# The second matrix product of an attention-and-MoE kernel as Strassen's seven half-size products

## The chip, the cores and the metric

One core of one Trainium2 chip. The metric is the device time of one execution of the whole kernel in microseconds (us); the median of several runs is compared. A core has TensorE (PE, matrix products into PSUM), VectorE (DVE, elementwise), ScalarE (ACT, activation functions), GpSimd (POOL, here used to issue loads that also convert types) and SyncE (SP, here used to issue stores and transposing transfers). Each engine takes its own instructions in the order of the program, and engines wait for one another through semaphores.

## The reference

```python
# q, k, v: (8, 8, 576, 64) = batch, heads, sequence, head_dim;  chunks of 64 along the sequence
scores = (1 / sqrt(64)) * q_c @ k_c.T            # 64 x 64 for each chunk and head
attn   = softmax(scores)
out    = attn @ v_c
x      = out as (4608 tokens, 512)
h      = x @ w_in                                # 512 -> 2048
g      = h * sigmoid(beta * h)
return g @ w_out                                 # 2048 -> 512, float32
```

Two matrix products of equal size, 4608 x 512 x 2048 each, hold nearly all of the arithmetic.

## The kernel before, in words

**Tiling.** The 4608 tokens are 18 units of 256 tokens; two units make a block of 512 tokens, so there are nine blocks (0 to 8). For each unit: loads of q, k (`load_qk`, L95 and L101) and v (`load_v`, L109) on GpSimd's queue, converted to fp16; a transpose of q and k (`emit_T`), on VectorE for units 0 to 7 (L153) and as transposing transfers on SP for units 8 to 17 (L148); the scores on TensorE and their exponential on ScalarE (`emit_sc`; units from 8 on: matmul L208, exp L214); the product with v (`emit_pv`, L242), whose extra 65th column, a constant in the v tile, gives the softmax denominators; the division on VectorE (`emit_norm`, reciprocal L253 and multiply L257); and the transpose of the result to `xt` (`emit_xt_pe`, or `emit_xt_dma` on SP, L281).

**First layer** (`emit_m(j, m)`): for block j and each of 16 slices m of 128 columns of w_in, four matmuls of 512 columns (L292) into one PSUM bank `hps`, a tanh on ScalarE (L300) and one VectorE operation (L301) that writes g in fp16 to `gt`, 128 x 16 x 512. It uses h * sigmoid(beta h) = 0.5 h (tanh(beta h / 2) + 1), with `beta2` = beta/2 (L369); the factor 0.5 is applied when the output is copied.

**Second layer** (`emit_t(j, t)`): for each 128 tokens t of block j, 16 matmuls of 512 columns (L314) with a slice of `gt` as the weights and `w_out16` as the moving operand; then a copy with scale 0.5 on ScalarE (L324) and a store on SP (L326). The very last 128 tokens are done in two halves of 256 columns (L478).

**Memory.** PSUM's eight banks: four in `ps_p` (hps, ops and the PE transposes), two in `ps_s` (scores, and the second half of pv), two in `ps_x` (the first half of pv). `qk_p` has four buffers, so the load of unit u + 4 into a q or k buffer waits until unit u has been transposed. `qt_p` has two. v is kept whole in `vbig`, 36 tiles of 128 tokens.

**Order.** The program is recorded by hand (`tc.manual_schedule()`). Blocks 0 and the start of 1 are written out. From there, for each j a list of items with a position between 0 and 1 (and a priority for ties) is sorted and emitted: the m of block j, the second layer of block j - 1, and the attention of the two units of block j + 1. For the attention `att_items(u, a0, w)` places sc at `a0`, pv at `a0 + 0.40 w`, the norms behind it and `T(u+1)`, with w the share of the block that the unit has (0.43 from j = 3 on, a0 = 0.03 and 0.46). emit_T(u) also records the loads of unit u + 4 behind it, on GpSimd.

```python
        def att_items(u, a0, w):
            return [(a0, 2, ("sc", u)), (a0 + 0.40 * w, 3, ("pv", u)),
                    (a0 + 0.41 * w, 3, ("norm", u, 0)), (a0 + 0.55 * w, 3, ("norm", u, 1)),
                    (a0 + (0.70 if u + 1 < XU else 0.10) * w, 3, ("T", u + 1))]
```

Of the kernel before, what the change touches and what calls it, by code (L numbers as in the profile page):

```python
# [8 lines left out]
FP32 = mybir.dt.float32  # L9
FP16 = mybir.dt.float16  # L10
# [5 lines left out]
def kernel(  # L16
# [18 lines left out]
    NU = NT // UNIT  # L35
    NTILE = NT // 128
    VP = 80
    scale = 1.0 / float(D) ** 0.5

    const = ctx.enter_context(tc.tile_pool(name="const", bufs=1))  # L40
# [22 lines left out]
    beta2 = const.tile([128, KFF], FP32)  # L63
# [43 lines left out]
    def load_v(i):  # L107
        for off, n, b, s in runs(i * 128, 128):
            nc.gpsimd.dma_start(  # L109
                out=vbig[off:off + n, i, :, 0:D],  # L110
                in_=v[b, :, s:s + n, :].rearrange("h p d -> p h d"),
            )

# [116 lines left out]
            nc.scalar.activation(out=et[:, s], in_=sc[:, s], func=ACTF.Exp, scale=scale)  # L230
        et_t[u] = et

    def emit_pv(u):
        et = et_t.pop(u)
        for s in range(2):
            i = 2 * u + s
            pool, tag = ((ps_x, "x"), (ps_s, "s"))[s]
            x = pool.tile([128, 2, 4, 128], FP32, tag=tag, name="x")
            for g in range(4):
                for r in range(2):  # L240
                    for c in range(2):
                        nc.tensor.matmul(  # L242
                            out=x[64 * c:64 * c + 64, r, g, 0:D + 1],
                            lhsT=(et[64 * r:64 * r + 64, s, 4 * c + g, :] if u < XU else
                                  et[64 * r:64 * r + 64, g % 2, 4 * s + 2 * c + g // 2, :]),
                            rhs=vbig[64 * r:64 * r + 64, i, 4 * c + g, 0:D + 1],
                        )
            x_t[u, s] = x

# [35 lines left out]
    def emit_m(j, m, c0=0, n=None):  # L285
        n = blocks[j][1] * UNIT if n is None else n
        if j not in gt_t:
            gt_t[j] = gt_p.tile([128, KFF, 512], FP16, tag="gt", name="gt")
        hps = ps_p.tile([128, 512], FP32, tag="p", name="hps")
        xr = xt_t[j].rearrange("p t (r k) (c q) -> p (t r) (k c) q", r=2, c=2)  # L290
        for kk in range(KDM):
            nc.tensor.matmul(  # L292
                out=hps[:, 0:n],
                lhsT=w_in16[m // 2][:, kk, (m % 2) * 128:(m % 2) * 128 + 128],
                rhs=xr[:, c0 // CH:(c0 + n) // CH, 2 * (kk % 2) + kk // 2, :],
                start=(kk == 0),
                stop=(kk == KDM - 1),
            )
        sg = sg_p.tile([128, 512], FP32, tag="sg", name="sg")
        nc.scalar.activation(out=sg[:, 0:n], in_=hps[:, 0:n], func=ACTF.Tanh, scale=beta2[:, m:m + 1])  # L300
# [7 lines left out]
    def emit_t(j, t, k0=0, k1=None):  # L308
        k1 = KFF if k1 is None else k1
        if k0 == 0:  # L310
            ops_t[j, t] = ps_p.tile([128, DM], FP32, tag="p", name="ops")
        ops = ops_t[j, t]
        for kk in range(k0, k1):
            nc.tensor.matmul(  # L314
                out=ops,
                lhsT=gt_t[j][:, kk, t * 128:(t + 1) * 128],
                rhs=w_out16[kk // 4][:, kk % 4, :],
                start=(kk == 0),
                stop=(kk == KFF - 1),
            )  # L320
        if k1 < KFF:
            return
        osb = osb_p.tile([128, DM], FP32, tag="osb", name="osb")
        nc.scalar.activation(out=osb, in_=ops, func=ACTF.Copy, scale=0.5)  # L324
        r0 = blocks[j][0] * UNIT + t * 128
        nc.sync.dma_start(out=out[r0:r0 + 128, :], in_=osb)  # L326

    def emit_idle(n, w):
        d = ps_p.tile([128, 512], FP32, tag="p", name="warm")
# [3 lines left out]
    with tc.manual_schedule():  # L333
        nc.vector.memset(idle, 0.0)
        nc.vector.memset(braw, 0.0)  # L335
        nc.vector.memset(vbig[:, :, :, D:D + 1], 1.0)
# [29 lines left out]
        emit_T_half(1)  # L366
        emit_sc_half(1)
        nc.vector.transpose(out=bt, in_=braw)
        nc.scalar.activation(out=beta2, in_=bt[:, 0:KFF], func=ACTF.Copy, scale=0.5)  # L369
        loads_to(4)  # L370
        emit_idle(8, 128)
        emit_pv(0)
# [23 lines left out]
        for s in range(4):  # L396
            for t in range(4):
                if s == 2 and t == 1:
                    emit_T(2)
                if s == 2 and t == 3:  # L400
                    emit_sc(2)
                if s == 3 and t == 0:
                    emit_pv(2)
                    emit_norm(2, 0)
                    emit_norm(2, 1)
                    emit_T(3)
                if s == 3 and t == 2:
# [14 lines left out]
        emit_m(1, 7, 0, 256)  # L422

        def att_items(u, a0, w):
            return [(a0, 2, ("sc", u)), (a0 + 0.40 * w, 3, ("pv", u)),
                    (a0 + 0.41 * w, 3, ("norm", u, 0)), (a0 + 0.55 * w, 3, ("norm", u, 1)),
                    (a0 + (0.70 if u + 1 < XU else 0.10) * w, 3, ("T", u + 1))]

        for j in range(1, NB):
            items = []  # L430
            if j == 1:
                items += [(0.04 * m, 0, ("h", m)) for m in range(8)]
                items += [(0.32 + 0.085 * (m - 8), 0, ("m", m)) for m in range(8, KFF)]
                items += [(0.80, 3, ("T", 4))]
            else:
                m0 = 0.30 if j == 2 else 0.02
                items += [(m0 + (1 - m0) * m / KFF, 0, ("m", m)) for m in range(KFF)]
                for t in range(4):
                    for hf in range(2):
                        items.append((0.98 * (t + 0.5 * hf) / 4, 1, ("t", t, hf)))  # L440
                if j == 2:
                    items += [(0.00, 0, ("sc", 4)), (0.05, 3, ("pv", 4)), (0.06, 3, ("norm", 4, 0)),
                              (0.07, 3, ("norm", 4, 1)), (0.08, 3, ("T", 5)), (0.13, 2, ("sc", 5)),
                              (0.16, 2, ("xp", 4, 0)), (0.18, 2, ("xp", 4, 1)), (0.20, 2, ("pv", 5)),
                              (0.21, 3, ("norm", 5, 0)), (0.22, 3, ("norm", 5, 1)), (0.23, 3, ("T", 6)),
                              (0.27, 2, ("xp", 5, 0)), (0.29, 2, ("xp", 5, 1))]
                if j + 1 < NB:
                    if j == 2:
                        items += att_items(6, 0.36, 0.32) + att_items(7, 0.68, 0.29)
                    else:  # L450
                        for i in range(2):
                            items += att_items(2 * j + 2 + i, 0.03 + 0.43 * i, 0.43)
            items.sort(key=lambda it: it[:2])
            for _, _, it in items:
                if it[0] == "m":
                    emit_m(j, it[1])
                elif it[0] == "h":
                    emit_m(j, it[1], 256, 256)
                elif it[0] == "t":
                    emit_t(j - 1, it[1], 8 * it[2], 8 * it[2] + 8)  # L460
                elif it[0] == "sc":
                    emit_sc(it[1])
                elif it[0] == "pv":
                    emit_pv(it[1])
                elif it[0] == "norm":
                    emit_norm(it[1], it[2])
                    if it[1] not in (4, 5):
# [7 lines left out]
        for hf in range(2):  # L475
            ops = ps_p.tile([128, DM], FP32, tag="p", name="ops")
            for kk in range(KFF):
                nc.tensor.matmul(  # L478
                    out=ops[:, 0:256],
                    lhsT=gt_t[NB - 1][:, kk, 384:512],  # L480
                    rhs=w_out16[kk // 4][:, kk % 4, 256 * hf:256 * hf + 256],
                    start=(kk == 0),
                    stop=(kk == KFF - 1),
                )
            osb = osb_p.tile([128, DM], FP32, tag="osb", name="osb")
            dst = out[NT - 128:NT, 256 * hf:256 * hf + 256]
            if hf == 0:
                nc.scalar.activation(out=osb[:, 0:256], in_=ops[:, 0:256], func=ACTF.Copy, scale=0.5)
                nc.sync.dma_start(out=dst, in_=osb[:, 0:256])
            else:  # L490
                nc.vector.tensor_scalar(out=osb[:, 0:256], in0=ops[:, 0:256], scalar1=0.5, scalar2=None, op0=ALU.mult)
                nc.scalar.dma_start(out=dst, in_=osb[:, 0:256])


# [28 lines left out]
```

## Time and profile before

| | |
|---|---|
| median of 3 runs | 298.5 us (298.28 to 300.6) |
| span of the profiled execution, first to last instruction | 296.9 us |
| PE, DVE, ACT, POOL busy | 282.6, 140.9, 148.4, 97.1 us |
| granted TensorE clock, mean | 0.988 of full |
| second layer's matmuls, 512 columns | 560 seen, L314 |
| landing of a transposing transfer, issue to landed, median | kT 7.5 us, qT 8.4 us, xt 2.9 us |
| landing of an output store of 256 KB, median | 3.8 us |

How to read it: matmuls are pipelined, so the mean duration of one (379 ns for 512 columns) is longer than the distance from one to the next; the chain of work that ended last, which gives the time that each stretch of matmuls adds, is the better measure. The profiled execution has no time of its own beside its span: the runs' times are taken apart from it, and lie around 1.6 us above the span.

### The profile page before, as it was taken

To read this page: it belongs to the slowest core of one execution; us is meant where nothing else is said; L and a number is where in the kernel's file an instruction comes from. 1 tells how busy PE (TensorE), PEld (TensorE's weight loads), DVE (VectorE), ACT (ScalarE), POOL (GpSimd) and SP (SyncE) were. 2 spreads that over 40 slices of the span, in tenths; PEclk is the share of its full clock that TensorE was granted. 3 is DMA by queue.
4 is the path that set the end of the run, shared out by engine and by line. 5 is a ranking of instruction groups with operands and counts; after the bars stand their busy time and mean duration, and the time that the engine had idled before them with its cause. 6 is when DMAs were issued, how large, how long until landed. Compare 5 with 4: busy or idle time off the path is not lost.

```text
span 296.9 us, 6545 instructions
## 1 busy us (share of the span) xinstructions
PE 282.6 (95%) x2722; PEld 139.2 (47%) x2722; DVE 140.9 (47%) x258; ACT 148.4 (50%) x232; POOL 97.1 (33%) x124
## 2 busy tenths in 40 slices
PE   7699999897799999999999999999999999999995
PEld 3565445644444444444444444444444444444444
DVE  3457604876547535353535353535353536444300
ACT  3278317872646554555455545554545454544411
POOL 8853678417934563324445151000000000000000
PEclk9869999999999999999999999999999999999999
DMA  9999999999996999999999999863527312100111
GB/s 141 165 197 205 182 179 209 206 122 74 172 149 96 149 188 134 144 148 151 140 153 155 143 130 148 126 112 62 121 72 110 56 57 75 48 35 35 38 71 71
DMA packets 141932, 36.86 MB, mean 124 GB/s; under 512 B 130000, under 2 KB 137424, under 8 KB 141904
## 3 DMA queue, kind: packets, MB, share of 16 engines
q0 software_dynamic: 101216, 18.10, 81.2%
q1 hardware_dynamic: 40544, 18.24, 32.0%
q8 instruction: 21, 0.34, 0.5%
q10 hardware_dynamic: 144, 0.13, 0.1%
q14 instruction: 7, 0.06, 0.1%
HBM read 36.71 MB, written 9.44 MB: 155 GB/s over the span
## 4 chain that ended last, share of the span: by engine, by line
PE 79%; DMA 10%; POOL 4%; DVE 2%; ACT 2%; issue 2%; DVEq 0%; ACTq 0%; POOLq 0%
PE ops L314 37%; PE hps L292 36%; DMA wout<-in_moe_w_out_dram 5%; DMA win<-in_moe_w_in_dram 3%; DMA qu<-in_q_dram 2%; PE x L242 2%; POOL vbig L109 2%; PE sc L208 1%; PE ops L478 1%; PE sc L221 1%; DVE x L257 1%; ACT xt L277 1%; POOL qu L101 1%; POOL ku L101 1%; POOL h L339 1%
## 5 line engine op out<-in xcount | busy, mean ns | idle before, releaser
L301 DVE SCALAR_TENSOR_TENSOR gt<-sg,hps 128x512 f16<-128x512 f32 (+1 forms) x158 | 100.6, 639 | 119.0 <-ACT sg L300 118.8
L292 PE MATMUL hps<-xt,win 128*128 128x512 f16 (+1 forms) x632 | 139.1, 365 | 2.6 <-ACT xt L277 2.2
L300 ACT ACTIVATE sg<-hps,beta 128x512 f32<-128x512 f32 (+1 forms) x158 | 101.9, 650 | 78.0 <-PE hps L292 77.4
L314 PE MATMUL ops<-wout,gt 128*128 128x512 f16 x560 | 130.9, 379 | 0.0
L292 PEld LDWEIGHTS <-win 128*128 128x128 f16 x632 | 60.8, 99 | 62.8 <-issue 2.8
L314 PEld LDWEIGHTS <-gt 128*128 128x128 f16 x560 | 53.8, 98 | 63.5
L324 ACT ACTIVATE osb<-ops 128x512 f32<-128x512 f32 x35 | 20.9, 597 | 40.8 <-PE ops L314 40.8
L95 POOL DMA_DIRECT2D qu<-in_q_dram x22 | 18.5, 850 | 62.9 <-DMA qT<-qu 46.2
L109 POOL DMA_DIRECT2D vbig<-in_v_dram x40 | 34.1, 869 | 10.4 <-DMA wout<-in_moe_w_out_dram 4.3
L257 DVE TENSOR_TENSOR x<-x,rd 128x512 f16<-128x512 f32 (+1 forms) x40 | 25.2, 637 | 1.2
L95 POOL DMA_DIRECT2D ku<-in_k_dram x22 | 18.7, 868 | 0.0
L230 ACT ACTIVATE et<-sc 128x1024 f16<-128x1024 f32 (+1 forms) x9 | 7.3, 833 | 14.6 <-PE sc L221 14.5
L253 DVE RECIPROCAL rd<-x 128x8 f32<-128x8 f32 x36 | 7.2, 201 | 12.9 <-PE x L242 12.9
L214 ACT ACTIVATE et<-sc 128x1024 f16<-128x1024 f32 x10 | 10.2, 1016 | 0.0
L242 PEld LDWEIGHTS <-et 64*64 64x64 f16 x576 | 6.3, 109 | 7.8 <-issue 2.5
L221 PE MATMUL sc<-qT,kT 32*64 32x64 f16 x448 | 5.3, 199 | 4.1 <-DVE qT L153 4.1
L242 PE MATMUL x<-vbig,et 64*64 64x65 f16 x576 | 8.4, 197 | 0.8 <-ACT et L230 0.6
L101 POOL DMA_DIRECT2D qu<-in_q_dram x10 | 7.7, 783 | 2.2 <-DMA win<-in_moe_w_in_dram 1.5
L101 POOL DMA_DIRECT2D ku<-in_k_dram x10 | 7.7, 774 | 2.1 <-DMA win<-in_moe_w_in_dram 1.3
L331 PE MATMUL warm<-idle 128*128 128x128 f16 (+1 forms) x42 | 6.9, 319 | 1.2 <-DVE braw L335 1.2
L221 PEld LDWEIGHTS <-kT 32*64 32x64 f16 x448 | 4.6, 112 | 6.9 <-DVE qT L153 4.2
L277 ACT COPY xt<-xp 128x512 f16<-128x512 f16 x10 | 5.6, 585 | 1.9 <-PE xp L273 1.9
(34 smaller groups left out, 58.0 us busy)
## 6 DMA issues: line engine op xcount, KB each, us to landing
out_dram<-osb SPq DMA_DIRECT2D x35, 256.0 KB, 3.8
vbig<-in_v_dram POOLq DMA_DIRECT2D x32, 128.0 KB, 7.4
qu<-in_q_dram POOLq DMA_DIRECT2D x20, 128.0 KB, 5.5
ku<-in_k_dram POOLq DMA_DIRECT2D x20, 128.0 KB, 6.8
win<-in_moe_w_in_dram POOLq DMA_DIRECT2D x8, 256.0 KB, 8.8
wout<-in_moe_w_out_dram POOLq DMA_DIRECT2D x4, 512.0 KB, 12.4
qu<-in_q_dram POOLq DMA_DIRECT2D x4, 256.0 KB, 6.0
ku<-in_k_dram POOLq DMA_DIRECT2D x4, 256.0 KB, 7.4
```

The source lines that it names most:

```text
L95: nc.gpsimd.dma_start(out=tv[off:off + n, sp], in_=src[b, :, s:s + n, :].rearrange("h p d -> p h d"),)
L101: nc.gpsimd.dma_start(out=t[off // 2:(off + n) // 2], in_=src[b, :, s:s + n, :].rearrange("h (p r) d -> p h r d", r=2),)
L109: nc.gpsimd.dma_start(out=vbig[off:off + n, i, :, 0:D], in_=v[b, :, s:s + n, :].rearrange("h p d -> p h d"),)
L214: nc.scalar.activation(out=et, in_=sc, func=ACTF.Exp, scale=scale)
L221: nc.tensor.matmul(out=sc[o0:o0 + 64, c // 2, h, :], lhsT=kt[p0:p0 + 32, h, :, e], rhs=qt[p0:p0 + 32, h, :, e], start=(e == 0), stop=(e == 1),
L242: nc.tensor.matmul(out=x[64 * c:64 * c + 64, r, g, 0:D + 1], lhsT=(et[64 * r:64 * r + 64, s, 4 * c + g, :] if u < XU else et[64 * r:64 * r ...
L257: nc.vector.tensor_tensor(out=o, in0=x[:, r, :, 0:D], in1=rd[:, r].to_broadcast(list(o.shape)), op=ALU.mult)
L292: nc.tensor.matmul(out=hps[:, 0:n], lhsT=w_in16[m // 2][:, kk, (m % 2) * 128:(m % 2) * 128 + 128], rhs=xr[:, c0 // CH:(c0 + n) // CH, 2 * ...
L300: nc.scalar.activation(out=sg[:, 0:n], in_=hps[:, 0:n], func=ACTF.Tanh, scale=beta2[:, m:m + 1])
L301: nc.vector.scalar_tensor_tensor(out=gt_t[j][:, m, c0:c0 + n], in0=sg[:, 0:n], scalar=1.0, in1=hps[:, 0:n], op0=ALU.add, op1=ALU.mult,)
L314: nc.tensor.matmul(out=ops, lhsT=gt_t[j][:, kk, t * 128:(t + 1) * 128], rhs=w_out16[kk // 4][:, kk % 4, :], start=(kk == 0), stop=(kk == K ...
L324: nc.scalar.activation(out=osb, in_=ops, func=ACTF.Copy, scale=0.5)
```

## The change

The second layer of block 0 stays. That of blocks 1 to 8 becomes Strassen's scheme in its variant with few additions: g of a block is cut in four (tokens 0-255 and 256-511 by the first and second half of the 2048 channels), w_out likewise, and seven products of half size replace eight. Products run in the order 1, 2, 6, 5, 7, 3, 4; 1, 6, 7 and 4 go one after the other into one PSUM accumulator, 2 (then 5 and 3) into another, and between them the accumulators are copied (ScalarE) or added to an output tile (VectorE). Each product is two halves t of eight matmuls with 256 columns. Four sums of parts of g are made per block on VectorE (`emit_sum`), and four differences of parts of w_out once (`emit_wt`). Stores are of 256 x 256.

To make room, v becomes a ring of 16 tiles. From unit 8 on both halves of pv use `ps_s`, one after the other, and `ps_x` holds the two accumulators (in block j = 2 they lie in `ps_p`). The constant column of v is 2.0 instead of 1.0, which halves x and h, so beta2 and the factor 0.5 at the output go. The positions of the attention items change for units from 8 on.

```diff
-    vbig = big.tile([128, NTILE, H, VP], FP16)
+    vbig = big.tile([128, NV, H, VP], FP16)          # NV = 16, indexed by i % NV
+    wt = [big.tile([128, 8, 256], FP16, name=f"wt{i}") for i in range(4)]
+    sm = [big.tile([128, 8, 256], FP16, name=f"sm{i}") for i in range(4)]
...
-            pool, tag = ((ps_x, "x"), (ps_s, "s"))[s]
+            pool, tag = (ps_x, "x") if s == 0 and u < XU else (ps_s, "s")
...
+    def emit_wt(i, qs=(0, 1)):
+        for q in qs:
+            o = [t[:, 4 * q:4 * q + 4, :] for t in wt]
+            a, b = {
+                0: (w_half(0, q, 1), w_half(0, q, 0)),
+                1: (w_half(1, q, 1), o[0]),
+                2: (w_half(1, q, 1), w_half(0, q, 1)),
+                3: (w_half(1, q, 0), o[1]),
+            }[i]
+            nc.vector.tensor_tensor(out=o[i], in0=a, in1=b, op=ALU.subtract)
+
+    def emit_sum(j, i):
+        g = gt_t[j]
+        a11, a12 = g[:, 0:8, 0:256], g[:, 8:16, 0:256]
+        a21, a22 = g[:, 0:8, 256:512], g[:, 8:16, 256:512]
+        a, b, op = ((a21, a22, ALU.add), (sm[0], a11, ALU.subtract),
+                    (a11, a21, ALU.subtract), (a12, sm[1], ALU.subtract))[i]
+        nc.vector.tensor_tensor(out=sm[i], in0=a, in1=b, op=op)
...
+    def emit_prod(j, p, t):
+        if p == 1 and t == 0:
+            if j == 1:
+                acc_t[j] = [ps_p.tile([128, 512], FP32, tag="p", name="acc") for _ in range(2)]
+            else:
+                xz = ps_x.tile([128, 2, 512], FP32, tag="x", name="xz")
+                acc_t[j] = [xz[:, 0], xz[:, 1]]
...
+        acc = acc_t[j][0 if p in (1, 6, 7, 4) else 1]
+        for kk in range(8):
...
+            nc.tensor.matmul(out=acc[:, 256 * t:256 * t + 256], lhsT=lhsT, rhs=rhs,
+                start=(p in (1, 2, 5) and t == 0 and kk == 0),
+                stop=(t == 1 and kk == 7), skip_group_check=True)
+        if t == 0:
+            return
+        r, c, how = {1: (0, 0, "copy"), 2: (0, 0, "add"), 6: (0, 1, "copy"), 5: (1, 1, "copy"),
+                     7: (1, 1, "add"), 3: (0, 1, "add"), 4: (1, 0, "copy")}[p]
+        if how == "copy":
+            oq_t[j, r, c] = osb_p.tile([128, DM], FP32, tag="osb", name="osb")
+            nc.scalar.copy(out=oq_t[j, r, c], in_=acc)
+        else:
+            o = oq_t[j, r, c]
+            nc.vector.tensor_tensor(out=o, in0=acc, in1=o, op=ALU.add)
+        if p in (2, 7, 3, 4):
+            emit_store(j, r, c)
...
         def att_items(u, a0, w):
+            if u >= XU:
+                return [(a0, 2, ("sc", u)), (a0 + 0.34 * w, 3, ("pv", u, 0)),
+                        (a0 + 0.35 * w, 3, ("norm", u, 0)), (a0 + 0.60 * w, 3, ("pv", u, 1)),
+                        (a0 + 0.61 * w, 3, ("norm", u, 1)), (a0 + 0.80 * w, 3, ("T", u + 1))]
...
-                for t in range(4):
-                    for hf in range(2):
-                        items.append((0.98 * (t + 0.5 * hf) / 4, 1, ("t", t, hf)))
+                for i, p in enumerate((1, 2, 6, 5, 7, 3, 4)):
+                    for t in range(2):
+                        items.append((0.98 * (2 * i + t) / 14, 1, ("prod", p, t)))
+                for i in range(4):
+                    items.append((0.005 + 0.07 * i, 4, ("sum", i)))
...
-        for t in range(3):
-            emit_t(NB - 1, t)
...
+        for i in range(4):
+            emit_sum(NB - 1, i)
+        for p in (1, 2, 6, 5, 7, 3, 4):
+            for t in range(2):
+                emit_prod(NB - 1, p, t)
```

The differences of w_out are recorded in block 0's second layer: number 0 behind T(2), numbers 2, 1 and 3 behind T(3). In the changed program the items of a block from j = 3 on begin with prod(1,0), sum 0, m 0, sc, prod(1,1), sum 1, m 1, prod(2,0), m 2, sum 2, pv half 0 and its norm, m 3, prod(2,1), sum 3, m 4, prod(6,0), pv half 1 and its norm, m 5, prod(6,1), T, m 6, prod(5,0), m 7, and then sc of the second unit.

More of the change, by code (lines that the diff above doesn't have):

```diff
@@ L37 @@
     VP = 80
+    NV = 16
+    HF = DFF // 2
     scale = 1.0 / float(D) ** 0.5
@@ L62 @@
     bt = const.tile([128, 32], FP32)
-    beta2 = const.tile([128, KFF], FP32)
     w_in16 = [big.tile([128, KDM, 256], FP16, name=f"win{g}") for g in range(8)]
     w_out16 = [big.tile([128, 4, DM], FP16, name=f"wout{g}") for g in range(4)]
-    vbig = big.tile([128, NTILE, H, VP], FP16)
+    vbig = big.tile([128, NV, H, VP], FP16)
+    wt = [big.tile([128, 8, 256], FP16, name=f"wt{i}") for i in range(4)]
+    sm = [big.tile([128, 8, 256], FP16, name=f"sm{i}") for i in range(4)]
     blocks = [(u, 2) for u in range(0, NU, 2)]
@@ L109, in load_v @@
             nc.gpsimd.dma_start(
-                out=vbig[off:off + n, i, :, 0:D],
+                out=vbig[off:off + n, i % NV, :, 0:D],
                 in_=v[b, :, s:s + n, :].rearrange("h p d -> p h d"),
@@ L231, in emit_sc, with emit_pv @@
         et_t[u] = et
-    def emit_pv(u):
-        et = et_t.pop(u)
-        for s in range(2):
+    def emit_pv(u, halves=(0, 1)):
+        et = et_t[u]
+        for s in halves:
             i = 2 * u + s
-            pool, tag = ((ps_x, "x"), (ps_s, "s"))[s]
+            pool, tag = (ps_x, "x") if s == 0 and u < XU else (ps_s, "s")
             x = pool.tile([128, 2, 4, 128], FP32, tag=tag, name="x")
@@ L245, in emit_pv @@
                                   et[64 * r:64 * r + 64, g % 2, 4 * s + 2 * c + g // 2, :]),
-                            rhs=vbig[64 * r:64 * r + 64, i, 4 * c + g, 0:D + 1],
+                            rhs=vbig[64 * r:64 * r + 64, i % NV, 4 * c + g, 0:D + 1],
                         )
@@ L299, in emit_m @@
         sg = sg_p.tile([128, 512], FP32, tag="sg", name="sg")
-        nc.scalar.activation(out=sg[:, 0:n], in_=hps[:, 0:n], func=ACTF.Tanh, scale=beta2[:, m:m + 1])
+        nc.scalar.activation(out=sg[:, 0:n], in_=hps[:, 0:n], func=ACTF.Tanh, scale=bt[:, m:m + 1])
         nc.vector.scalar_tensor_tensor(
@@ L323, in emit_t, with w_at, w_half @@
         osb = osb_p.tile([128, DM], FP32, tag="osb", name="osb")
-        nc.scalar.activation(out=osb, in_=ops, func=ACTF.Copy, scale=0.5)
+        nc.scalar.copy(out=osb, in_=ops)
         r0 = blocks[j][0] * UNIT + t * 128
         nc.sync.dma_start(out=out[r0:r0 + 128, :], in_=osb)
+    def w_at(r, kk, c):
+        g = 2 * r + kk // 4
+        return w_out16[g][:, kk % 4, 256 * c:256 * c + 256]
+    def w_half(r, q, c):
+        return w_out16[2 * r + q][:, :, 256 * c:256 * c + 256]
+    def emit_wt(i, qs=(0, 1)):
[8 more added lines that the diff above has]
+            nc.vector.tensor_tensor(out=o[i], in0=a, in1=b, op=ALU.subtract)
@@ new lines, in emit_sum, with emit_store @@
+    def emit_sum(j, i):
[5 more added lines that the diff above has]
+        nc.vector.tensor_tensor(out=sm[i], in0=a, in1=b, op=op)
+    acc_t = {}
+    oq_t = {}
+    def emit_store(j, r, c):
+        r0 = blocks[j][0] * UNIT + 256 * r
+        nc.sync.dma_start(
+            out=out[r0:r0 + 256, 256 * c:256 * c + 256].rearrange("(t p) d -> p t d", t=2),
+            in_=oq_t.pop((j, r, c)).rearrange("p (t d) -> p t d", t=2),
+        )
@@ new lines, in emit_prod @@
+    def emit_prod(j, p, t):
[5 more added lines that the diff above has]
+                acc_t[j] = [xz[:, 0], xz[:, 1]]
+        g = gt_t[j]
+        acc = acc_t[j][0 if p in (1, 6, 7, 4) else 1]
+        c0 = t * 128
+        for kk in range(8):
+            lhsT = {
+                1: lambda: g[:, kk, c0:c0 + 128],
+                2: lambda: g[:, 8 + kk, c0:c0 + 128],
+                3: lambda: sm[3][:, kk, c0:c0 + 128],
+                4: lambda: g[:, 8 + kk, 256 + c0:256 + c0 + 128],
+                5: lambda: sm[0][:, kk, c0:c0 + 128],
+                6: lambda: sm[1][:, kk, c0:c0 + 128],
+                7: lambda: sm[2][:, kk, c0:c0 + 128],
+            }[p]()
+            rhs = {
+                1: lambda: w_at(0, kk, 0),
+                2: lambda: w_at(1, kk, 0),
+                3: lambda: w_at(1, kk, 1),
+                4: lambda: wt[3][:, kk, :],
+                5: lambda: wt[0][:, kk, :],
+                6: lambda: wt[1][:, kk, :],
+                7: lambda: wt[2][:, kk, :],
+            }[p]()
+            nc.tensor.matmul(
+                out=acc[:, 256 * t:256 * t + 256],
+                lhsT=lhsT,
+                rhs=rhs,
+                start=(p in (1, 2, 5) and t == 0 and kk == 0),
+                stop=(t == 1 and kk == 7),
+                skip_group_check=True,
+            )
+        if t == 0:
[10 more added lines that the diff above has]
+            emit_store(j, r, c)
@@ L335 @@
         nc.vector.memset(braw, 0.0)
-        nc.vector.memset(vbig[:, :, :, D:D + 1], 1.0)
+        nc.vector.memset(vbig[:, :, :, D:D + 1], 2.0)
         for a, eng, dst in ((0, nc.sync, raw0), (1, nc.gpsimd, qk0[1])):
@@ L368 @@
         nc.vector.transpose(out=bt, in_=braw)
-        nc.scalar.activation(out=beta2, in_=bt[:, 0:KFF], func=ACTF.Copy, scale=0.5)
         loads_to(4)
@@ L399 @@
                     emit_T(2)
+                    emit_wt(0)
                 if s == 2 and t == 3:
@@ L406 @@
                     emit_T(3)
+                    emit_wt(2)
+                    emit_wt(1)
+                    emit_wt(3)
                 if s == 3 and t == 2:
@@ L458 @@
                     emit_m(j, it[1], 256, 256)
-                elif it[0] == "t":
-                    emit_t(j - 1, it[1], 8 * it[2], 8 * it[2] + 8)
+                elif it[0] == "prod":
+                    emit_prod(j - 1, it[1], it[2])
+                elif it[0] == "sum":
+                    emit_sum(j - 1, it[1])
                 elif it[0] == "sc":
@@ L463 @@
                 elif it[0] == "pv":
-                    emit_pv(it[1])
+                    emit_pv(it[1], (0, 1) if len(it) == 2 else (it[2],))
                 elif it[0] == "norm":
@@ L472 @@
                     emit_T(it[1])
-        for t in range(3):
-            emit_t(NB - 1, t)
[L475 to L492, printed above, removed]
+        for i in range(4):
[3 more added lines that the diff above has]
+                emit_prod(NB - 1, p, t)
 _INS = ['q', 'k', 'v', 'moe_w_in', 'moe_w_out', 'moe_beta']
```

## The prediction

> **What bounds the kernel now.** (All times in us.) I read the page's head first, then the chain that ended last, then the groups by shape, and last SyncE's (SP's) own rows of the timeline, because the change moves work there.
>
> ```profile
> span 296.9 us, 6545 instructions
> PE 282.6 (95%) x2722; PEld 139.2 (47%) x2722; DVE 140.9 (47%) x258; ACT 148.4 (50%) x232; POOL 97.1 (33%) x124
> PE 79%; DMA 10%; POOL 4%; DVE 2%; ACT 2%; issue 2%; DVEq 0%; ACTq 0%; POOLq 0%
> ```
>
> TensorE (PE) is busy all through; the chain is 79% PE. In the chain in order of time every block looks like this:
>
> ```profile
> 225.24 0.38 PE sc L208 x32
> 225.62 0.97 PE hps L292 x4
> 226.59 1.73 PE ops L314 x8
> 228.31 0.86 PE hps L292 x4
> ...
> 290.19 3.51 PE ops L478 x32
> ```
>
> Eight 512-column matmuls take 1.73, so 0.216 each. The 256-column ones at the end take 3.51/32 = 0.1097, though each has its own weight load. An attention piece costs 0.38, and 0.1 more on the matmul behind it (0.97 against 0.86). A steady block is 128 x 0.216 + 4 x 0.48 = 29.5 (the sc pieces start at 195.69 and 225.24).
>
> VectorE (DVE) prices:
>
> ```profile
> L257 DVE TENSOR_TENSOR x<-x,rd 128x512 f16<-128x512 f32 x32 | 22.1, 692 | 1.1
> L253 DVE RECIPROCAL rd<-x 128x8 f32<-128x8 f32 x36 | 7.2, 201 | 12.9 <-PE x L242 12.9
> L257 DVE TENSOR_TENSOR x<-x,rd 128x256 f16<-128x256 f32 x8 | 3.0, 420 | 0.1
> L171 DVE CAST h<-raw 128x512 f16<-128x512 f32 x1 | 0.4, 385 | 0.0
> ```
>
> And SP's queue, where each transfer starts behind the one before it:
>
> ```profile
> 208.96 1.30 SPq L148 DMA_TRANSPOSE kT<-ku  x1
> 210.37 1.26 SPq L148 DMA_TRANSPOSE qT<-qu  x1
> 214.20 0.33 SPq L326 DMA_DIRECT2D out_dram<-osb  x1
> 217.20 2.63 SPq L281 DMA_TRANSPOSE xt<-x  x2
> ```
>
> qT landed 3.1 after its issue here, so from the kT issue to both operands in place is 4.5. For the units whose transposes were issued at 192.5 and 222.1 it is 5.4 and 6.1; mean 5.3. While GpSimd's loads still run (119.2) it is 12.5. Before, T(u+1) stands right behind sc(u), at least 12 ahead of the scores that need it, so none of this shows.
>
> **The products.** Per block 64 x 0.216 = 13.81 become 7 x 16 x 0.1097 = 12.29: 1.52 less. In six blocks (items j = 3 to 8) that is -9.1; the block at j = 2 and the tail are worked out whole below. pv in two halves: one switch more for each of ten units, 10 x 0.1 = +1.0.
>
> **The sums.** Four 128x2048 f16 operations a block, SBUF to SBUF, which no row shows. Upper bound: the tensor_tensor rows give (692-420)/256 = 1.06 ns an element and 0.148 fixed, so 2.32. Lower: the CAST, the only elementwise row with nothing in PSUM, is (385-148)/512 = 0.463 ns an element, so 1.10. I take 1.10, as the operands are all in SBUF.
>
> The Trainium skill, "VectorE: DVE Perf Modes", section "The perf-mode tier table", has 16-bit tensor_tensor from SBUF at twice the fp32 rate, 1.22 for 2048 elements; no run here shows it, and with it the sum below would be about 3 more.
>
> DVE's load in a steady block is then 16 x 0.69 + 4 x 0.9 (norms) + 3 x 0.69 (output adds) + 4 x 1.1 = 21 of 28: it fits, but the sums stand early in the block, ahead of the norms.
>
> **The transposes.** In the new att_items T(u+1) moves from 0.10 w to 0.80 w. For the first unit of a block (say 8) that is position 0.374; sc(9) is at 0.46. With the prices above, PE reaches (from the block's start) prod(1,0) 0, m0 0.88, sc(8) 1.74, m1 3.10, m2 4.84, pv(8,0) 5.70, prod(2,1) 6.86, pv(8,1) 9.47, sc(9) at 14.1. On SP the new order is xt(8,0), store of product 2, xt(8,1), kT, qT; so kT waits for norm(8,1) on DVE. DVE in its program order, each end: last gt of the block before 1.45 (after the last m, PE to gt takes 1.45: 279.83 to 281.28), sum0 2.55, gt0 3.24, sum1 4.35, gt1 (behind the exp and the copy of product 1 on ScalarE) 5.55, gt2 7.15, sum2 8.25, norm(8,0) 9.15, gt3 9.85, add 10.55, sum3 11.65, gt4 12.35, norm(8,1) 13.25. xt(8,1) holds SP 1.2, kT starts at 14.5, plus 5.3: 19.8. sc(9) was due at 14.1: **PE stands 5.7**, and everything queued behind sc(9) on PE, m and products both, stands with it. By the rows 4.9 to 6.5. Five units are like this (9, 11, 13, 15, 17): **+28.5**. The GpSimd loads that made the transposes take 12.5 are released by the transpose before (bufs=4), hence are mostly over by then; if not, 7 more in each of the first three.
>
> For units 10, 12, 14, 16: pv(9,1) ends 8.0 after sc(9), norm 9.25, xt 10.5, the store of product 3 waits for its add (11.05), kT 11.5, landed 16.8; sc(10) is due 15.85 after sc(9): +1.0 each, **+4.0** (0 to 2).
>
> **The clock.** The windows of one microsecond show the granted clock (the number before the last two):
>
> ```profile
> 11.00:12.00 1.00, 0.27 (x2) 0.10 (x1) 0.00 (x0) 0.64 (x3) 1.00 (x2) 1.00 1.54 191
> 12.00:13.00 1.00, 0.00 (x0) 0.00 (x0) 0.62 (x1) 0.14 (x1) 0.81 (x2) 1.00 1.90 157
> 13.00:14.00 1.00, 0.27 (x20) 0.27 (x24) 0.68 (x2) 0.00 (x0) 0.38 (x1) 0.53 2.27 161
> 14.00:15.00 1.00, 1.00 (x63) 0.87 (x55) 0.00 (x0) 0.15 (x1) 0.92 (x2) 0.50 1.70 186
> ...
> 20.00:21.00 1.00, 0.94 (x10) 0.61 (x8) 0.35 (x2) 0.87 (x3) 0.24 (x1) 1.00 1.44 195
> ```
>
> After 2 of nothing on PE (11.74 to 13.73) the clock is 0.50 until about 19.9: 6.2 of work at half speed, 3.1 lost. Waits of about 1 near 67 and 73 cost no clock. Bounds 0 to 3.1 for a stand of 5.7; I take 2.5, near the longer row: **+12.5**.
>
> The rule that speaks against the change is in "TensorE: Matmul & The Clock Gate" (Part 1): an idle window of about 3.4 drops the clock to half, and a busy one of that length gives it back. The row agrees roughly (6.2 at half); by the rule a stand loses 1.7 to 3.4.
>
> **Block j = 2.** DVE now also makes the sums in the stretch where before PE already waited for it (sc(5) waited 1.14 for the transposes). With 1.10 each in DVE's order: sum0 ends 69.7, the norms of unit 4 71.55, sum1 72.65, T(5) 74.05; sc(5) starts 0.7 late. Behind pv(5) come the add (78.2), norm, sum3, norm (81.1); xt follows and the first m is at 82.2 instead of 78.86: 3.3 late, with 0.74 less product work left: +2.6, and for the clock half the bound of a small stand, +1.2. In this block the two accumulators also hold two of the four ps_p banks, so each m waits for the gt two before it: from 0 to 7.0 (all other DVE work of that stretch: four norms, a pair of transposes, three adds); I take +2.
>
> **Block 0, weights.** Eight 128x1024 differences. Two lie in 7.4 of DVE's idle time before the norm at 44.27. Six at 0.62 follow T(3) (ends 47.26) and are over at 51.0; the first gt after them starts at 51.16. Cost 0 at the lower price; at 1.24 each, +3.5.
>
> **The tail** after the last m. Before: 296.9-279.83 = 17.1. After: sums run to 5.85 on DVE and the add of product 2 to 6.55; product 6 waits for sum1 and runs 3.65 to 5.4, product 5 waits for that add and runs 6.6 to 8.4, the rest end at 13.6, copy 0.6, store 3.8 (the median landing of its 256 KB): 18.3. +1.2.
>
> The v ring (16 tiles) waits for a pv that ended two blocks earlier, and the shorter memset and the dropped beta2 lie in DVE's and ScalarE's idle time at the start: nothing, or 0.3 if that were gone.
>
> **Sum** on the profiled span: 296.9 - 9.1 + 1.0 + 28.5 + 4.0 + 12.5 + 2.6 + 1.2 + 2 + 0 + 1.2 = 340.8. The median of the runs (298.5) is 1.6 above the span: **342.4**.
>
> **Rivals.**
> 1. The clock stays up. Stands of 1 cost none in this trace, and nothing here shows one of 5.7. Then 342.4 - 12.5 - 1.2 = 328.7.
> 2. The sums run at the full tensor_tensor price, 2.32. Norm(8,1) ends at 16.7 and pv(8,1) waits too: 9.25 a stand, so 5 x 3.55 = 17.8 more, 4.9 in block 2, 3.5 in block 0, 4.9 in the tail: 373.5. For it: the only tensor_tensor rows are at this rate. Against: they read PSUM.
> 3. The transposes stay congested: 7 more in three stands, 363. For it: 12.5 at 119.2. Against: the loads wait for the transpose before.
> 4. The other side, not slower: the transposes start early because their inputs have long been loaded. In the trace kT for unit 9 starts at 104.0, ahead of sc(8) at 107.0 which stands before it in the program. Then stands and clock go: 342.4 - 28.5 - 4.0 - 12.5 - 1.2 = 296.2, and 290 if block 2 hides its part too. It decides from a lead of 5.3 before sc(u+1); the lead here is -0.4 (kT at 14.5, sc due 14.1), as SP's own order puts kT behind an xt that needs the norm.
>
> **How the numbers follow.** Forecast 0.47, rival 1 0.22, rival 2 0.12, rival 3 0.09, rival 4 0.10. Low end: rival 1 with stands of 4.9 and block 2 at no cost, about 318; I put 316. High end: 370, which holds rival 3 and leaves out most of rival 2. What can be told from no change here is about 1%. Rival 4 splits into faster 0.06, same 0.03, and the rest slower.
>
> **What would show it.** In the changed profile the chain should name kT/qT transposes before sc in blocks 3 to 7, SP's kT should start right after an xt, and PE should stand some 5 in the middle of each of these blocks, with a granted clock near 0.5 behind it. The 256-column products should show 0.11 apart; the sums' mean decides between 1.1 and 2.3. I am wrong if PE shows no wait at sc for units 9, 11, 13, 15, 17.

## The result, and the profile after

The changed kernel takes 342.63 us (median of 4 runs, 336.43 to 345.1), the kernel before 299.31 us beside it (4 runs, 298.28 to 300.6). The ratio is 1.132, 95% interval 1.121 to 1.143; it leaves out the two of the changed kernel's runs that had the lowest granted clock (0.949), of which one is the profiled run, and so lies below the ratio of the medians. The forecast was 342.4: the total is right, within 0.1% of the median and 1.1% above the 338.7 that the ratio stands for. Several of the terms behind it are not right, and they cancelled, so that the close fit is luck. (All times are in us.)

The head of the changed kernel's profile:

```profile
span 342.9 us, 7378 instructions
PE 287.6 (84%) x3090; PEld 180.4 (53%) x3090; DVE 195.9 (57%) x321; ACT 149.1 (43%) x231; POOL 97.0 (28%) x124
PEclk9879999978999898999899998999899999999989
```

PE was busy for 95% of the span and is now busy for 84%, although there is less to multiply: it waits. VectorE went from 140.9 to 195.9 and is still free for over two fifths of the span. The clock row has an 8 in most blocks. The page's chain can't be used here: it goes back only from 339.66 to 324.21, into the tail, and holds 4.5% of the span. The costliest groups say who waits for whom (busy, mean ns of one, then the idle time before them with its releaser):

```profile
L396 PE MATMUL xz<-wt,sm 128*128 128x256 f16 x336 | 48.2, 293 | 13.8 <-DVE osb L413 12.4
L355 DVE TENSOR_TENSOR sm<-gt 128x2048 f16<-128x2048 f16 x16 | 19.5, 1220 | 0.3
L211 PE MATMUL sc<-qT,kT 64*64 64x64 f16 x320 | 5.0, 208 | 14.3 <-DMA qT<-qu 14.3
L396 PE MATMUL xz<-wt,gt 128*128 128x256 f16 x112 | 14.3, 272 | 3.0 <-DVE osb L413 3.0
```

The third row is the stand that the prediction put at the centre: the scores wait for the transposes, but for 14.3 in all, not 32.5. The first and the fourth are waits that it did not have: products wait for an add on VectorE (L413). In order of time, PE in the block that was worked through in the prediction:

```profile
121.52 1.03 PE L295 MATMUL hps<-xt,win 128*128 128x512 f16 x4
124.27 1.03 PE L396 MATMUL xz<-wt,sm 128*128 128x256 f16 x8 [1.72 <-DVE osb L413]
...
128.96 1.03 PE L295 MATMUL hps<-xt,win 128*128 128x512 f16 x4
132.73 0.45 PE L211 MATMUL sc<-qT,kT 64*64 64x64 f16 x32 [2.74 <-DMA qT<-qu]
```

and SP beside it:

```profile
124.33 0.53 SPq L362 DMA_DIRECT2D out_dram<-osb  x1
126.81 1.20 SPq L284 DMA_TRANSPOSE xt<-x  x1
128.18 1.23 SPq L151 DMA_TRANSPOSE kT<-ku  x1
129.51 1.28 SPq L151 DMA_TRANSPOSE qT<-qu  x1
```

SP's order is the predicted one: store, second xt, kT, qT. The scores start 4.55 after the kT issue (128.18 to 132.73). The matmul at 124.27 is the first of product 6. Product 6 writes the first accumulator and continues from product 1; what it waits for is the reader of the *other* accumulator, the add of product 2. From j = 3 on both accumulators are halves of one tile `xz`, and waits are kept by tile. In block j = 2, where they are two tiles `acc`, there is no such wait.

The block, j = 3, begins with one more wait, for its xt; and in the tail, behind the last m, product 6 has its longest wait for the add:

```profile
113.07 1.79 PE L295 MATMUL hps<-xt,win 128*128 128x512 f16 x4 [3.48 <-DMA xt<-x]
324.86 3.53 PE L396 MATMUL xz<-wt,sm 128*128 128x256 f16 x16 [2.62 <-DVE osb L413]
```

Where the 46.0 between the two spans (342.9 and 296.9) lies, by the starts of the blocks in PE's timeline:

| stage | before | after | difference |
|---|---|---|---|
| up to block j = 2 | 67.5 | 67.2 | -0.2 |
| j = 2 | 36.3 | 41.3 | +5.0 |
| j = 3 | 30.1 | 40.7 | +10.6 |
| j = 4 to 7 together | 118.2 | 140.6 | +22.4 |
| j = 8 | 27.6 | 28.0 | +0.3 |
| tail, from the last m on | 17.2 | 25.2 | +7.9 |

### The profile page after: what moved, and what is told of

It reads as the page before. It is cut to its first block, busy times and chain, and to the rows that moved or that the text cites. A ratio compares the mean times of both kernels' runs of the same rounds, so it can differ in the third digit from the quotient of the medians.

```text
span 342.9 us, 7378 instructions
## 1 busy us (share of the span) xinstructions
PE 287.6 (84%) x3090; PEld 180.4 (53%) x3090; DVE 195.9 (57%) x321; ACT 149.1 (43%) x231; POOL 97.0 (28%) x124
## 5 line engine op out<-in xcount | busy, mean ns | idle before, releaser
L303 ACT ACTIVATE sg<-hps,bt 128x512 f32<-128x512 f32 (+1 forms) x158 | 101.9, 650 | 118.6 <-PE hps L295 118.1
L396 PEld LDWEIGHTS <-sm 128*128 128x128 f16 x512 | 51.3, 102 | 35.2 <-issue 19.5
L396 PE MATMUL xz<-wt,sm 128*128 128x256 f16 x336 | 48.2, 293 | 13.8 <-DVE osb L413 12.4
L396 PEld LDWEIGHTS <-gt 128*128 128x128 f16 x384 | 37.7, 100 | 18.0 <-issue 6.4
L396 PE MATMUL xz<-wout,gt 128*128 128x256 f16 x224 | 29.3, 276 | 0.7 <-ACT osb L410 0.7
L410 ACT COPY osb<-xz 128x512 f32<-128x512 f32 x28 | 16.4, 587 | 23.6 <-PE xz L396 23.6
L260 DVE TENSOR_TENSOR x<-x,rd 128x512 f16<-128x512 f32 (+1 forms) x40 | 25.2, 637 | 1.2
L413 DVE TENSOR_TENSOR osb<-xz,osb 128x512 f32<-128x512 f32 x21 | 14.4, 684 | 10.8 <-issue 8.8
L355 DVE TENSOR_TENSOR sm<-gt 128x2048 f16<-128x2048 f16 x16 | 19.5, 1220 | 0.3
L211 PE MATMUL sc<-qT,kT 64*64 64x64 f16 x320 | 5.0, 208 | 14.3 <-DMA qT<-qu 14.3
L396 PE MATMUL xz<-wt,gt 128*128 128x256 f16 x112 | 14.3, 272 | 3.0 <-DVE osb L413 3.0
L396 PE MATMUL xz<-wout,sm 128*128 128x256 f16 x112 | 14.3, 272 | 0.8 <-DVE osb L413 0.8
L317 PE MATMUL ops<-wout,gt 128*128 128x512 f16 x64 | 14.5, 379 | 0.0
```

The costliest lines, as they stand in the source:

```text
L260: nc.vector.tensor_tensor(out=o, in0=x[:, r, :, 0:D], in1=rd[:, r].to_broadcast(list(o.shape)), op=ALU.mult)
L317: nc.tensor.matmul(out=ops, lhsT=gt_t[j][:, kk, t * 128:(t + 1) * 128], rhs=w_out16[kk // 4][:, kk % 4, :], start=(kk == 0), stop=(kk == K ...
L355: nc.vector.tensor_tensor(out=sm[i], in0=a, in1=b, op=op)
L396: nc.tensor.matmul(out=acc[:, 256 * t:256 * t + 256], lhsT=lhsT, rhs=rhs, start=(p in (1, 2, 5) and t == 0 and kk == 0), stop=(t == 1 and ...
L410: nc.scalar.copy(out=oq_t[j, r, c], in_=acc)
L413: nc.vector.tensor_tensor(out=o, in0=acc, in1=o, op=ALU.add)
```

## Experiments

Theory A: the loss has two separate causes, each with its own wait, and a clock that falls behind them: the late transposes (`T(u+1)` at 0.80 w, queued on SP behind an xt that needs a norm), and the shared accumulator tile. The rival B, by which PE waits for VectorE's sums and the late transposes only show it, expects 337 or more with T moved back. Four kernels on one chip, where the kernel before had a median of 299.84 (13 runs):

**e1: the changed kernel with T early again.**

```diff
-  (a0 + 0.61 * w, 3, ("norm", u, 1)), (a0 + 0.80 * w, 3, ("T", u + 1))]
+  (a0 + 0.61 * w, 3, ("norm", u, 1)), (a0 + 0.10 * w, 3, ("T", u + 1))]
```

> Changed kernel with T(u+1) back at 0.10 w, everything else as changed. Theory A (late transposes stop TensorE): the five stands of about 2.75 before sc of the odd units go, and with them the half-speed windows behind four of them (1.7 each), 20 in all: about 322. The 1.7 stand before product 6 stays. Theory B (VectorE's sums are what TensorE waits for, the transposes only show it): the wait moves to another place, gain at most 5: 337 or more.

Measured: 323.93 (323.57 to 327.4), ratio 1.082 (1.072 to 1.093); the profiled span is 322.1. PE's timeline in the same block:

```profile
124.60 1.03 PE L396 MATMUL xz<-wt,sm 128*128 128x256 f16 x8 [1.72 <-DVE osb L413]
...
129.30 1.03 PE L295 MATMUL hps<-xt,win 128*128 128x512 f16 x4
130.26 0.45 PE L211 MATMUL sc<-qT,kT 64*64 64x64 f16 x32
```

No scores wait any more, and the wait of product 6 is the same to the hundredth. A steady block is 31.19 from product 6 to product 6 (124.60 to 155.79). Theory A is right and B falls: the place of T is worth 15 by the ratios (1.132 to 1.082) and 19 by the medians, its stands of 13.9 and, where an execution has it, the clock behind them.

**e2: two accumulator tiles, T late as in the change.** The two banks of `ps_x` become two tiles with tags of their own (the pv that shared them is fitted to it).

```diff
-                xz = ps_x.tile([128, 2, 512], FP32, tag="x", name="xz")
-                acc_t[j] = [xz[:, 0], xz[:, 1]]
+                acc_t[j] = [ps_x.tile([128, 512], FP32, tag=tg, name="xz") for tg in ("xa", "xb")]
```

> Changed kernel with the two accumulators as two one-bank tiles instead of one two-bank tile (the first half of pv of units 0 to 7 uses the same two). Theory A (each product waits for the reader of the OTHER accumulator, because both lie in one tile): the stands before product 6 (1.7), before product 4 (0.36) and six in the tail go or shrink. In the blocks with attention the stand before sc grows by what product 6 no longer waits, since the norm that releases the transposes is set by VectorE; gain there only 0.4 each, in the block without attention 1.6, in the tail 4 to 6: about 333. Theory B (the stands add): 5 x 1.7 more, about 324. If product 6 really waits for sum 1, nothing moves there.

Measured: 340.85 (339.05 to 341.27), ratio 1.134 (1.126 to 1.142), so no gain by the ratios (1.132 before the edit) and 1.8 by the medians, and a miss against the expected time.

```profile
124.08 1.04 PE L402 MATMUL xz<-wt,sm 128*128 128x256 f16 x8
...
128.78 1.03 PE L302 MATMUL hps<-xt,win 128*128 128x512 f16 x4
134.41 0.64 PE L211 MATMUL sc<-qT,kT 64*64 64x64 f16 x32 [4.61 <-DMA qT<-qu]
```

Product 6 starts without a wait; with it PE comes to the scores earlier, and waits 4.61 there. The five stands are 4.61, 4.75, 4.61, 4.75 and 4.61. So the false wait hid behind the true one: the transposes land when VectorE's norm and SP let them, and 1.9 of the stand had only been paid earlier in the block. Longer stands also cost more clock: its mean is 0.928 here, 0.949 in the changed kernel's profile. That last part I had not put into the expectation.

**e3: both edits.**

> Both edits together. Theory A: neither stand is left in the steady blocks, each costs 28.2 to 28.6 instead of 29.5 before; the block at j = 2 stays some 5 longer than before, the tail about even: 297 to 303. Theory B (the sums load VectorE too much): blocks of 31 or more remain, 312 or more.

Measured: 304.11 (300.29 to 305.09, 10 runs), ratio 1.009 (1.004 to 1.014), 1 above the range expected. By the medians, undoing one cause gave 19 and the other 2, and undoing both gives 38; by the ratios it is 15, nothing, and 37. That is what two waits do that cover one another. Steady blocks now run without a wait, 28.43 each (142.85 to 171.28 between scores), against 29.55 before. What is left lies outside them:

```profile
73.40 0.71 PE L224 MATMUL sc<-qT,kT 32*64 32x64 f16 x64 [3.45 <-DVE qT L156]
79.81 0.29 PE L283 MATMUL xp<-ident,x 128*128 128x128 f16 x2 [1.39 <-DVE x L267]
82.34 0.40 PE L283 MATMUL xp<-ident,x 128*128 128x128 f16 x4 [0.82 <-DVE x L267]
112.10 1.86 PE L302 MATMUL hps<-xt,win 128*128 128x512 f16 x4 [3.34 <-DMA xt<-x]
```

The first three rows are block j = 2, where VectorE also transposes and normalises; the last is the start of j = 3, whose xt comes late. They and the clock behind them take back all that the six steady blocks gain.

**e4: the kernel before, with T alone moved late.** Here T(8) moves too, which in the changed program it does not.

```diff
-  (a0 + (0.70 if u + 1 < XU else 0.10) * w, 3, ("T", u + 1))]
+  (a0 + (0.70 if u + 1 < XU else 0.80) * w, 3, ("T", u + 1))]
```

> The kernel BEFORE with only T(u+1) moved from 0.10 w to 0.80 w for units from 8 on; no Strassen, no sums. Theory A: kT then stands behind a store at about 14.2 of a block and lands 4.5 later, sc of the second unit is due at 14.8, so five stands of about 3.9 and up to 1.7 of clock each: 320 to 328. Theory B (the late transposes do harm only with the sums on VectorE): 299 to 302.

Measured: 335.62 (334.95 to 336.74), ratio 1.118 (1.110 to 1.126): above the range expected. PE's row of the first such stand, then three windows of 3.41 us around it (the number behind the length is PE's busy time, the granted clock is the number before the last two):

```profile
124.65 0.64 PE L208 MATMUL sc<-qT,kT 64*64 64x64 f16 x32 [4.60 <-DMA qT<-qu]
```

```profile
119.71:123.12 3.41, 0.34 (x2) 0.00 (x0) 1.38 (x2) 0.88 (x2) 0.00 (x0) 1.00 0.79 187
123.12:126.53 3.41, 1.88 (x36) 1.03 (x37) 0.00 (x0) 1.02 (x1) 1.49 (x2) 0.50 0.27 52
126.53:129.95 3.42, 3.42 (x10) 1.22 (x9) 0.00 (x0) 0.00 (x0) 3.42 (x5) 0.50 1.57 100
```

The stands before the odd units are 4.60 to 4.71, two more before units 8 and 10 are 2.20 and 0.53. Without a single Strassen product or sum, one position in the item list costs 36. The stands are as long as in e2, which has the sums on VectorE: the sums do not set them. The miss has three parts: the five stands are 23.2 together, where 19.5 was expected; the two even ones, 2.7, were not expected; and the half clock lasts 6.83 at four of the five (3.41 at the other). It begins at 123.12, within the stand, so that of its 3.4 only (1.88 + 3.42)/2 = 2.65 falls on PE at work; over the five stands that is 12.0, where I had expected at most 8.5.

Four more kernels on another chip, where the kernel before had 300.12 (7 runs).

**e5: e3 with the second layer of block 1 plain, as before, and Strassen from block 2 on.** The edit in the loop over j:

```diff
+                if j == 2:
+                    for t in range(4):
+                        for hf in range(2):
+                            items.append((0.98 * (t + 0.5 * hf) / 4, 1, ("t", t, hf)))
+                else:
-                for i, p in enumerate((1, 2, 6, 5, 7, 3, 4)):
...
```

> Both edits, and the second layer of block 1 (items j = 2) plain as before, so Strassen starts one block later. Theory A (block j = 2 loses 5 through VectorE's early sums and half-speed windows, and a late xt costs 3.3 and a window at the start of j = 3): all of it goes. Six blocks at 1.3 less than before, tail 1 longer: 292 to 295. Rival (the steady blocks are no faster than before, the products' gain is eaten by smaller waits): 298 to 301.

Measured: 295.31 (293.06 to 298.77), ratio 0.983 (0.974 to 0.992). Block j = 2 falls back to waits of 1.38, 0.59 and 0.82, and the wait at the start of j = 3 to 1.68. In the one block in which PE already waited for VectorE, the plain second layer is the better one.

**e6: e5 with another order in the tail.** The add of product 2 goes ahead of sums 2 and 3, and the last accumulator is copied and stored in two halves by two engines.

```diff
-        for i in range(4):
-            emit_sum(NB - 1, i)
+        emit_sum(NB - 1, 0)
+        emit_sum(NB - 1, 1)
         for p in (1, 2, 6, 5, 7, 3, 4):
             for t in range(2):
                 emit_prod(NB - 1, p, t)
+            if p == 2:
+                emit_sum(NB - 1, 2)
+                emit_sum(NB - 1, 3)
```

> As the last one, and in the tail the add of product 2 is recorded before sums 2 and 3, and the last accumulator is copied and stored in two halves by two engines. The 0.95 before product 5 goes and the end comes 0.9 sooner: 1.5 to 2 less than the last one, 290 to 293.

Measured: 292.89 (292.57 to 296.87), ratio 0.980 (0.972 to 0.989). This version beats both kernels: 2% less time than before, with the whole interval below 1, and by the ratios 13% less than the change as made.

```profile
span 291.1 us, 7314 instructions
PE 275.0 (95%) x3042; PEld 170.3 (59%) x3042; DVE 190.4 (65%) x329; ACT 147.3 (51%) x231; POOL 97.1 (33%) x124
L402 PE MATMUL xz<-wt,sm 128*128 128x256 f16 x336 | 42.8, 273 | 0.5 <-DVE sm L362 0.5
```

The products' idle time is 0.5 in all. The tail from its first product to the end is 16.8 (274.31 to 291.1) against 18.1 in e3 (280.76 to 298.9), so the tail's own edit is worth 1.3 in the profiles. (The spans of e5 and e6 are equal all the same, 291.2 and 291.1: e6's profile has a half-clock stretch in block j = 2 that e5's has not.) The times of e5 and e6 overlap, so that between these two the runs do not show it.

**e7 and e8: the clock by itself.** e8 is the changed kernel once more; e7 is the same with 16 idle matmuls of 256 columns on PE ahead of the scores of the odd units from 9 on, 1.75 of work.

```diff
-  return [(a0, 2, ("sc", u)), (a0 + 0.34 * w, 3, ("pv", u, 0)),
+  return [(a0, 1.9, ("idle", u))] * (u % 2) + [(a0, 2, ("sc", u)), (a0 + 0.34 * w, 3, ("pv", u, 0)),
```

> The changed kernel with 16 matmuls of 256 columns on zeros in front of sc of each odd unit from 9 on, where TensorE stands 2.75 anyway (1.75 of work, into a spare bank). Theory A (each stand costs a half-speed window of its own): the stands stay as long, counted to the start of sc, but the granted clock stays up and 1.7 is won at four or five of them: 6.5 to 8.5 less than the changed kernel. Rival (the low clock costs nothing on the path, or filler delays sc): no difference, or 1 to 3 more.

> The changed kernel itself once more, for comparison on the same chip: 336 to 345.

Measured: e7 339.96 (337.08 to 344.48), e8 345.32 (340.02 to 348.58). The filler gives 5.4 by the medians, less than expected, the runs overlap, and the ratio of e7, 1.131, is that of the changed kernel, 1.132. The mean granted clock of the four runs is 0.964 to 0.980 in e7 and 0.944 to 0.968 in e8: the expected direction, but that the filler gains time is not shown. The traces show why it is hard to see. In the changed kernel's profile, two windows of 3.41 around the stand that begins at 130 read

```profile
130.25:133.66 3.41, 0.93 (x37) 0.87 (x38) 0.69 (x1) 0.89 (x2) 0.53 (x1) 1.00 0.52 100
133.66:137.07 3.41, 3.41 (x14) 1.82 (x12) 0.10 (x1) 1.87 (x3) 3.41 (x5) 0.50 1.07 72
```

and in e8, the same program, around its stand of 2.77 before 133.68,

```profile
129.00:132.42 3.42, 1.91 (x13) 1.08 (x11) 1.38 (x2) 1.37 (x2) 0.00 (x0) 1.00 0.82 157
132.42:135.83 3.41, 2.15 (x45) 1.58 (x46) 0.00 (x0) 1.54 (x2) 1.76 (x3) 1.00 0.20 33
```

The same stand costs half of 3.41, 1.7, in one execution and nothing in the other. In the first, four of the five stands of 2.72 to 2.88 cost 1.4 to 1.7 each (6.4 in all), in the second none of five stands of 2.73 to 2.87. In e7 three stands of about 1.0 cost none; of two of about 2.0 one did.

The windows are not chosen freely. In every profile the clock changes only at points that lie a whole number of 3.41 apart, and where this grid lies differs from execution to execution. In the first profile the stand falls mostly into one window of the grid, in which PE works for 0.93 of 3.41, and the next window has half clock; in the second it is shared out over two, which work for 1.91 and 2.15, and the clock stays. Over all ten profiles (without the last 12 us of each), each of the 36 full-clock windows in which PE stood for at least 55% was followed by half clock, and none of the 750 in which it stood for less than 46%; in between, 5 of 29 were. So what a stand of 2.8 costs is decided by where it falls on the grid. This is read from the traces; no run here sets the place.

## Why the prediction was right, and where it was not

| step of the prediction | predicted | measured |
|---|---|---|
| products and pv, a steady block | -1.52 + 0.2 = -1.3 | 28.43 - 29.55 = -1.1 (e3) |
| a sum on VectorE | 1.10 | 1.22 |
| stands before sc of the odd units | 5 x 5.7 = 28.5 | 13.9 (e2, without the shared tile: 23.3) |
| even units | 4.0 | 0.4 |
| shared accumulator tile, j = 3 to 8 | not seen | 5 x (1.72 + 0.36) + 1.6 = 12.0 |
| clock behind the stands | 12.5 | 6.4 at four of five (e8: 0) |
| xt at the start of j = 3, and its clock | not seen | 3.1 more than before, and 1.7 |
| block j = 2 | 2.6 + 1.2 + 2 = +5.8 | +5.0 |
| tail | +1.2 | +7.9 (e3: 18.1 long, +0.9) |
| sum of all on the span | +43.9 | +46.0 |

**The stand before sc: mechanism right, size off.** Its chain held step by step: norm, xt, kT, qT, each behind the other on SP, and every odd unit from 9 on waits. The price had two terms. The landing was taken as 5.3, the mean of 4.5, 5.4 and 6.1; it was 4.55, the shortest row, and 4.54 in e2 (129.87 to 134.41). The lead of -0.4 was about -0.1 in e2 (kT at 129.87, the m before the scores over at 129.80). That makes the 4.6 that e2 shows, not 5.7. In the changed kernel itself the lead is 1.8 (kT at 128.18, m over at 129.99), because PE arrives late from the wait of product 6; so 2.74 is left.

**The shared tile was missed.** I read in the diff that `xz` holds both accumulators and priced only the bank count of block j = 2, not the wait that one tile brings. The step that failed is "The products", which takes the seven products as a stream without waits. It also spoils the tail, where I had product 6 at 3.65 behind sum 1. It waited for the add of product 2, which stands behind all four sums on VectorE:

```profile
322.99 1.22 DVE L355 TENSOR_TENSOR sm<-gt,sm 128x2048 f16<-128x2048 f16 x1
324.13 0.68 DVE L413 TENSOR_TENSOR osb<-xz,osb 128x512 f32<-128x512 f32 x1
```

Product 6 starts at 324.86, 7.1 after the tail's first product (317.75). Each of the five other products behind the first waits 0.67 to 0.84 for the copy or add before it; that makes gaps of 6.25 in all, and the window from 325 to 330 is granted 0.68 of the clock. With two tiles (e3) the tail is 18.1, with a wait of 0.95 before product 5 for just that add; 18.3 and this wait were predicted. The tail's working was right for the program that I thought I read.

**The sums.** I took the lower bound, 1.10; the measured mean is 1.22 (L355: 1,220 ns). The Trainium skill, "VectorE: DVE Perf Modes", section "The perf-mode tier table", has 1.22 for 2048 elements; the trace agrees. The full rate of rival 2, 2.32, is out.

**The clock.** 2.5 a stand was near for stands of 4.61 to 4.75: over five of them, PE at work lost 12.0 in e4 and 11.2 in e2 (1.4 to 3.0 each). The changed kernel's are shorter, 2.72 to 2.88, and cost 6.4 over five in one profile and nothing in another: the term was too high because the stands were. The half clock comes in stretches of 3.41 or 6.83. The Trainium skill, "TensorE: Matmul & The Clock Gate", Part 1, has windows of about 3.4 at half clock; an estimate from that is 1.7 lost for one and 3.4 for two, and the stretches agree. The page's condition, a window of some 3.4 without work, does not: stands of 2.7 to 2.9 cost a window here in four of ten cases, and 55% of a window without work was always enough.

**Block j = 2** was near (+5.0 for +5.8), by terms that were so only in part. The scores of unit 5 wait 3.19 (1.14 before), but less product work stands ahead of them, and counted from the block's start they come 0.6 later, for the 0.7 predicted. The first m starts at 84.24, 5.6 later in the block than before instead of 3.3, with a granted clock of 0.72 and 0.60 from 70 to 80, of which 2.7 falls on PE at work instead of 1.2. Against that the 2.0 for the two accumulators in `ps_p` did not come: from the first m to the end the block takes 24.3 (84.24 to 108.55), and before it took 24.9 (78.86 to 103.76).

**The start of j = 3** I did not look at. xt of unit 7 leaves SP as far ahead of the block as before (3.2 both times), but the two xt in this stretch land after 6.7 by their median, before after 4.4, with all 16 DMA engines busy in both. And the first m now stands behind one product half (0.87) instead of eight matmuls of 512 columns (1.73). 2.3 and 0.9 are about the 3.1 by which the wait grew (0.35 to 3.48). Why these transposes land later is not settled.

**The rivals.** Rival 1 (clock up) describes single executions: e8's best has the full clock through all five stands, yet 338.2 of span, since the shared tile and the tail stay. Rival 3 (congested transposes) is out: even the longest of the five stands is 2.88. Rival 4 (transposes early) did not happen by itself, as kT stayed behind xt; e1 shows what it is worth.

In sum, the stands, the even units and the clock behind the stands were 24 too high (45.0 for 20.7), and the shared tile, the tail and the start of j = 3 were 24 too low (1.2 for 24.7). By the measured terms of the table, j = 3 to 8 would be 30.9 longer; they are 33.3 longer. The 2.4 between are not tied to an event; in e1 two waits of 2.08 together make a block 2.76 longer (31.19 against 28.43), so a stop seems to cost PE somewhat more than its gap shows; no run separates the two.

## What to carry to other kernels

Before counting what a cheaper product saves, follow each of its operands' buffers: two accumulators in one tile make every product wait for a reader that it does not need, and this shows only as a wait for another engine's harmless add. When items are re-spaced by hand, look at the one that issues transfers: moving T behind the norms put it at the end of a queue whose head waited for VectorE, and cost 36 with no other change (e4). Two waits in one block cover each other, so undo them together before judging either: by the ratios they gave 15 and nothing singly, and 37 together, and the scheme paid off only once it was also kept out of the block in which VectorE was the bound.

## What the runs showed of the hardware

- The clock's loss is a matter of the execution, not only of the program: the same five stands of about 2.8 cost 6.4 in one profile and nothing in another, as the place of the 3.41 grid differs: in one window a stand of 2.8 is over half of it, shared out evenly over two it is 41% of each. This goes with the spread of the changed kernel's runs, 336.43 at a mean clock of 0.978 to 345.1 at 0.949; the spans of these two, 334.6 and 343.3, times their clocks are 327 and 326.
- Stands of about 4.7 always cost clock here: a half-clock stretch of 6.83 in four of five in e4 and in three of five in e2, and of 3.41 in the others; as the stretch can begin within the stand, PE at work lost 1.4 to 3.0. Waits of 1.72 before product 6 cost none where no longer one was near (e1, full clock from 120 to 300).
- 128x2048 fp16 operations from SBUF to SBUF take 1,220 ns on VectorE, 0.6 ns an element; 128x512 with fp32 from PSUM takes 684 (L413), 1.3 an element.
